# Values of a sliding-window attention: projected once per block of 128 tokens and copied to the overlapping key windows by DMA, instead of projected again for every window

## The chip, the core and the metric

The kernel runs on one core of a Trainium2 chip. The core has five engines that run side by side and meet only at semaphores: TensorE (PE, with its weight loads as PEld), VectorE (DVE), ScalarE (ACT), GpSimd (POOL) and SyncE (SP), which here only issues DMAs. Each engine works through its own instruction list in order, so an instruction that waits holds up everything behind it on that engine. The metric is the device time of one execution in microseconds (us), the median of several executions.

## The reference, cut to what matters

One transformer block with adaptive layer norm, 2048 tokens of 448 values, 16 heads of 28, bf16 inputs and outputs. Each token attends to itself and seven earlier tokens, two apart.

```python
mod = silu(c) @ w_mod                       # six rows of 448: sa, ca, ga, sb, cb, gb
h = layernorm(x) * (1 + ca) + sa
q, k, v = split(h @ wqkv)                   # 16 heads of 28
idx = pos[:, None] - arange(8) * 2          # masked where negative
o = softmax(q . k[idx] * 28**-0.5) . v[idx]
x = x + ga * (o @ wo)
h = layernorm(x) * (1 + cb) + sb
y = layernorm(h)
x = x + gb * (gelu(y @ w1 + b1) @ w2 + b2)  # hidden width 1792
```

## The kernel before, in words

**Layout.** Even tokens come first and odd tokens after them, so that the window of eight becomes eight neighbouring rows. The 2048 rows are 16 blocks of 128. `T.h` holds the normalized and modulated input transposed (four overlapping slices of the 448 channels on the partitions, tokens along the free axis), `T.q` and `T.k` the queries and keys in the same way.

**Attention.** Queries are cut into 36 groups of 57. A group needs 57 + 7 = 64 keys, so the key windows of neighbouring groups overlap by seven rows. Four groups make a *duo* (nine duos, `attention(d)`, line 676). In a duo, `lt` (line 694) multiplies keys and queries of all heads, `ex` (line 704, ACT) takes the exponential out of PSUM, `mk` (line 711, DVE) multiplies with a banded mask, `dn` (line 770) sums the weights, `pv` (line 783) multiplies them with the values, `ln` and `rc` (lines 793 and 798, ACT) make the reciprocal of the sum, and `on` (line 807, DVE) writes the result over the queries.

**Values before.** `v{d}` (lines 736 and 745) projects the values of a duo's four key windows straight onto the partitions where `pv` wants them: the window of 64 tokens is the stationary operand, so a matmul fills 64 of the 128 PSUM partitions, and two of them run beside each other at `tile_position=(0, 64 * u)`. That is 12 matmuls of 64 columns over 128 channels and 4 over the odd 64 channels, for two PSUM banks. `ve{d}.0` and `ve{d}.1` (line 294 through the helper `copy`, ACT) copy the two banks to the buffer `vb`, in which every head has 32 columns, of which the last four are zeroed once (`ebuf`). There are three `vb` buffers.

**The rest.** `qk` (lines 617 and 624, in `pair_mm`) projects queries and keys in pieces of 512 tokens. Blocks 0 to 7 are transposed by TensorE (`zt`, line 557), blocks 8 to 15 by a DMA transpose on SP (line 549). `wo` (line 823) and `x1` (line 832) add the attention to `x`; `norm2` makes the second and third layer norm on DVE, with a power on POOL (line 858) and an addition on POOL (`xp`, line 844), and transposes by DMA on SP (line 889). `w1` (lines 617 and 624), `gelu` (line 916, ACT), `w2` (line 929, the last block line 935) and `out` (line 946, DVE) are the MLP.

**The end.** The last block of 128 tokens is made in two halves of 224 columns, both in one PSUM tile, each with its own `out` and its own store (line 955).

**The start.** ACT issues three DMAs (part of `x`, two parts of `w_mod`), loads its function table and helps with the silu of `c`. POOL zeroes the padding and `wo`, makes the identity, the band mask (`mask1`) and its 16-fold copy (`mask`). `wo` has to be zeroed because only 28 of every 32 partitions are loaded. `fill` (line 466) are 28 matmuls of zeros which the planner puts wherever TensorE has nothing else.

**What sets the order.** Nothing is ordered by hand. Each piece of work is an item with its engine or engines, its dependencies and the buffers that it takes (`add`, line 77); PSUM is one pool of eight banks, `hm` one of three large buffers. `Plan.schedule` (line 107) plays the items through and, among those that can start, takes the one of highest priority; the priorities are a table of numbers per kind (`bias`) and per item (`delta`). The instruction list of each engine is the result. `phases` says which duos come before which quarters of the MLP: duos 0 to 6, quarters 0 and 1, duos 7 and 8, quarters 2 and 3. The exponential and the gelu need different ACT function tables, so ACT changes the table once per phase.

Of the kernel before, what the change touches and what calls it, by code (L numbers as in the profile page):

```python
# [66 lines left out]
class Plan:  # L67
# [162 lines left out]
CFG["tail"], CFG["slope"], CFG["window"] = 0.1512, 1.2963, 0.1  # L230
CFG["bias"] = {
    "bce": (-437.49, 11.669),
    "cst": (-315.02, 0.41),
    "dn": (-121.05, 0.55),
    "exp": (-590.42, 6.137),
    "gelu": (-217.98, 4.043),
    "h2": (-373.89, 0.036),
    "ln": (-583.27, 3.374),
    "lt": (72.47, 0.028),
    "md": (-377.14, 16.518),  # L240
    "mk": (54.22, 21.918),
    "mod2": (136.71, 0.694),
    "nm1": (32.99, 2.86),
    "nm2": (561.76, 2.811),
    "on": (169.44, 1.376),
    "out": (-413.48, 11.238),
    "pow1": (525.86, 1.379),
    "pow2": (-535.44, 0.028),
    "pv": (556.28, 40.0),
    "qk": (42.43, 17.816),  # L250
    "qke": (-395.64, 6.656),
    "rc": (-297.53, 6.437),
    "st1": (-388.63, 23.021),
    "st2": (24.1, 0.032),
    "store": (-563.5, 0.024),
    "v": (-393.34, 0.501),
    "ve": (573.27, 0.813),
    "w1": (-419.51, 24.455),
    "w2": (-582.63, 0.624),
    "w2s": (-527.88, 0.154),  # L260
    "wcp": (-38.96, 0.377),
    "wo": (-44.33, 40.0),
    "wos": (69.62, 2.823),
    "x1": (-248.35, 0.156),
    "xp": (-81.8, 6.268),
    "yt": (364.44, 0.134),
    "zt": (161.08, 0.071),
    "ztp": (-538.07, 0.138),
# [15 lines left out]
def build_plan(cfg):  # L284
# [13 lines left out]
    def memset(e, ap, c):  # L298
        T.eng[e].memset(ap, c)  # L299

    def psf(v):
        return T.ps[v.slot]

    def psb(v):
        return T.psb[v.slot]


    def fn(e):
# [5 lines left out]
    def load(name, nbytes, fn, wr, vals=(), n=1, q="SP", lag=0, lat=0.9, hold=()):  # L314
# [6 lines left out]
        it = add(name, "load", {q: 0.45 * n}, fn1, wr=wr, vals=vals, land=(lat, nbytes), after=after + list(hold))  # L321
        loads.append(it)
        return it
# [17 lines left out]

    def load_x(b0, n, q="SP", lag=0):
        def fn(e):
            return e.dma_start(out=T.x[:, b0:b0 + n, :], in_=xsrc(b0, n))
        return load(f"ldx{b0}", n * 128 * 896, fn, [("x", b) for b in range(b0, b0 + n)], q=q, lag=lag)

    def overl(dst, src, j, c0, c1):
        return dict(out=dst[:, 2 * j:2 * j + 2, 0:c1 - c0],
                    in_=src[192 * j:192 * j + 256, c0:c1].rearrange("(i p) n -> p i n", p=128))

    def fn(e):
        return e.dma_start(out=T.c_row[:], in_=T.c)
    load("ldc", 2000, fn, ["c_row"])
    load_x(0, 2, q="ACT")
    for i in range(3):
        def fn(e, i=i):
            w = wmod1()
            if i == 0:
                return e.dma_start(out=w[:, 0:2, :], in_=T.w_mod[0:256, 0:896].rearrange("(i p) n -> p i n", p=128))
            if i == 1:  # L360
                return e.dma_start(out=w[:, 3, :], in_=T.w_mod[320:448, 0:896])
            return e.dma_start(out=w[64:128, 2, :], in_=T.w_mod[256:320, 0:896])
        load(f"ldwmod1{i}", (256, 128, 64)[i] * 896 * 2, fn, [("wmod1", i)], vals=[fv], q=("SP", "ACT", "ACT")[i], lat=1.8)
    for j in range(2):
        def fn(e, j=j):
            return e.dma_start(**overl(T.Wv, T.wqkv, j, 896, 1344))
        load(f"ldwv{j}", 256 * 896, fn, [("Wv", j)])
    for j in range(2):
        def fn(e, j=j):
            return e.dma_start(**overl(wraw(), T.wqkv, j, 0, 896))  # L370
        load(f"ldwqk{j}", 256 * 896 * 2, fn, [("wraw", j)], vals=[fv])
    load_x(2, 2)
    load_x(4, 4)
    load_x(8, 4)
    for hh in range(2):
        for j in range(2):
            def fn(e, hh=hh, j=j):
                return e.dma_start(**overl(wmod2()[:, :, 896 * hh:896 * hh + 896], T.w_mod, j, 896 + 896 * hh, 1792 + 896 * hh))
            load(f"ldwmod2{hh}{j}", 256 * 896 * 2, fn, [("wmod2", hh, j)], vals=[wv], lag=3)
    for r in range(4):  # L380
        def fn(e, r=r):
            return e.dma_start(out=T.wo[32 * r:32 * r + DH, :, :],
                               in_=T.wo_d.rearrange("(m r e) n -> r e m n", r=4, e=DH)[r])
        load(f"ldwo{r}", 112 * 896, fn, [("wo", r)], lag=3)
    load_x(12, 4, lag=3)

    def fn(e):
        return e.dma_start(out=T.b1r[:], in_=T.b1.rearrange("(f p) -> f p", p=128))
    load("ldb1", 3600, fn, ["b1r"])

    def fn(e):
        return e.dma_start(out=T.b2[:], in_=T.b2_d.partition_broadcast(128))
    load("ldb2", 128 * 896, fn, ["b2"], lag=3)

    def fn(e):
        memset(e, T.zero[:], 0.0)
    add("zero", "cst", {"DVE": 0.3}, fn, wr=["zero"])

    def fn(e):
# [41 lines left out]
    def fn(e):  # L441
        memset(e, T.mask1[:], 1.0)
        for u in range(2):
# [4 lines left out]
                                      base=0, channel_multiplier=1)  # L448
    add("mask1", "cst", {"POOL": 1.0}, fn, wr=["mask1"])

    def fn(e):
        T.eng[e].tensor_copy(out=T.mask[:].rearrange("p (g c) -> p g c", c=SC),
                             in_=T.mask1[:].unsqueeze(1).to_broadcast([128, 16, SC]))
    add("mask", "cst", {"POOL": 1.0}, fn, rd=["mask1"], wr=["mask"])

    def fn(e):
        for t in T.vb:
            memset(e, t[:, :, :, DH:32], 0.0)
    add("ebuf", "cst", {"POOL": 0.9}, fn, wr=["ebuf"])


    fvl = val("ps", "fill")
    prev = None
    for i in range(cfg["nfill"]):
# [211 lines left out]
    def attention(d):  # L676
# [46 lines left out]
        def fn(e):  # L723
# [3 lines left out]
            def pos(P_, u):  # L727
                k0 = PADL + sub_tok(subs[P_][u]) - (WIN - 1)
                return k0
# [435 lines left out]
```

## Time and profile before

| what | us |
|---|---|
| median of three executions (lowest and highest) | 178.26 (177.97 to 179.09) |
| the profiled execution, its own time | 178.68 |
| its span, from the first to the last instruction | 177.0 |
| TensorE busy | 167.6 |
| DVE busy | 118.9 |
| ACT busy | 109.6 |
| POOL busy | 42.3 |

The profiled execution took 1.68 us more than its span, and 0.42 us more than the median. How to read the rows below: `ps<-Wv,hT` means that the tile `ps` (PSUM) was written from `Wv` and `hT`; `x108` is a count; a row of a timeline begins with the start and the length in us; what stands in brackets is how long the engine sat idle before it and what released it. The chain of waits is followed back from the last instruction to whatever released each one, and its rows give start and length in us. A busy TensorE is an upper bound, since the ends of pipelined matmuls are modelled, so its pace is better read from the distance of starts.

### The profile page before, as it was taken

Reading aid. Unit: us, or ns where it says so; the run is one execution under the profiler, and the core shown is the slowest. Engines: PE = TensorE matmul, PEld = TensorE weight load, DVE = VectorE, ACT = ScalarE, POOL = GpSimd, SP = SyncE. Lnnn points to the kernel's source line nnn. Section 1 sums busy time; section 2 is a strip of 40 time slices with the busy share of each in tenths; the row PEclk is TensorE's granted clock in tenths of the full one; section 3 lists DMA queues with packets and bytes.
Section 4 is the critical chain, followed back from the end, with each engine's and each line's share of the span. In section 5 each row is a group of like instructions: output and inputs, shape, how many; then the busy total and the mean of one; then the engine's idle time right before and its main releaser. Section 6 shows DMA issues by size and latency. Waiting matters only on the chain.

```text
span 177.0 us, 5323 instructions
## 1 busy us (share of the span) xinstructions
PE 167.6 (95%) x2243; PEld 83.3 (47%) x2243; DVE 118.9 (67%) x323; ACT 109.6 (62%) x203; POOL 42.3 (24%) x65
## 2 busy tenths in 40 slices
PE   7799996999899979999999999999999999999992
PEld 2457654344444453554434455555534455444571
DVE  3897898968989998999999906622785842200041
ACT  3077999969989987975567997802017820358100
POOL 7811320320415321101311102244241114200000
PEclk9999999999999999999999999999999999999999
DMA  5998384147986002000410400000221111300011
GB/s 163 375 365 272 123 166 80 32 93 214 327 255 81 4 17 52 4 0 4 89 30 11 98 15 4 6 0 27 83 104 30 31 28 31 107 0 0 0 67 37
DMA packets 23790, 15.13 MB, mean 86 GB/s; under 512 B 13909, under 2 KB 23766, under 8 KB 23766
## 3 DMA queue, kind: packets, MB, share of 16 engines
q1 hardware_dynamic: 23270, 14.22, 29.4%
q10 hardware_dynamic: 496, 0.57, 1.0%
q8 instruction: 17, 0.28, 0.6%
q14 instruction: 7, 0.06, 0.1%
HBM read 9.81 MB, written 1.84 MB: 66 GB/s over the span
## 4 chain that ended last, share of the span: by engine, by line
PE 78%; DVE 13%; ACT 3%; issue 2%; DMA 2%; POOL 0%; DVEq 0%; ACTq 0%
PE ps L617 29%; PE ps L929 23%; PE ps L823 7%; PE ps L624 6%; PE ps L736 4%; DVE z L541 3%; PE ps L783 2%; PE ps L694 2%; DVE et L711 2%; DVE st L523 2%; DMA x_all<-in_A_x_dram 2%; PE ps L935 2%; DVE qT L807 1%; ACT hT L589 1%; PE ps L770 1%
## 5 line engine op out<-in xcount | busy, mean ns | idle before, releaser
L916 ACT ACTIVATE hm<-ps,b1c 128x512 bf16<-128x512 f32 x56 | 34.3, 692 | 30.5 <-PE ps L624 26.4
L929 PE MATMUL ps<-w,hm 128*128 128x448 bf16 x210 | 40.9, 353 | 0.0
L617 PE MATMUL ps<-hT,w 128*128 128x512 bf16 x168 | 38.3, 380 | 0.0
L946 DVE TENSOR_TENSOR x_all<-ps,xp 128x448 bf16<-128x448 f32 (+1 forms) x17 | 10.0, 595 | 32.6 <-PE ps L929 30.5
L929 PEld LDWEIGHTS <-hm 128*128 128x128 bf16 x210 | 20.2, 98 | 18.8
L844 POOL TENSOR_TENSOR xp<-x_all,gbb 128x448 f32<-128x448 bf16 x16 | 17.0, 1063 | 39.7 <-DVE x_all L946 27.1
L617 PEld LDWEIGHTS <-w 128*128 128x128 bf16 x168 | 15.8, 98 | 20.7 <-issue 3.0
L858 POOL TENSOR_TENSOR rs<-tv,nhalf 128x2 f32<-128x2 f32 x16 | 12.4, 778 | 48.7 <-DVE tv L853 48.7
L617 PE MATMUL ps<-hT,Wqk 128*128 128x512 bf16 (+1 forms) x120 | 23.5, 337 | 0.0
L704 ACT ACTIVATE et<-ps 128x464 bf16<-128x464 f32 x36 | 18.1, 573 | 1.5 <-PE ps L694 1.5
L617 PEld LDWEIGHTS <-Wqk 128*128 128x128 bf16 x120 | 10.8, 98 | 9.7 <-issue 2.3
L711 DVE TENSOR_TENSOR et<-et,mask 128x928 bf16<-128x928 bf16 x18 | 11.0, 635 | 6.3 <-ACT et L704 6.2
L823 PE MATMUL ps<-wo,qT 128*128 128x448 bf16 x64 | 14.2, 354 | 1.0 <-DVE qT L807 1.0
L807 DVE TENSOR_TENSOR qT<-ps,rec 128x456 bf16<-128x456 f32 x18 | 11.3, 630 | 4.0 <-ACT rec L798 2.7
L736 PE MATMUL ps<-Wv,hT 128*64 128x448 bf16 x108 | 11.9, 357 | 0.0
L530 POOL TENSOR_TENSOR rs<-tv,nhalf 128x2 f32<-128x2 f32 x8 | 6.4, 804 | 20.8 <-DVE tv L526 20.5
L793 ACT ACTIVATE rec<-ps 128x464 f32<-128x464 f32 x18 | 10.0, 556 | 2.1 <-PE ps L770 2.1
L798 ACT ACTIVATE rec<-rec 128x464 f32<-128x464 f32 x18 | 10.6, 591 | 0.5
L832 DVE TENSOR_TENSOR x_all<-ps,x_all 128x448 bf16<-128x448 f32 x16 | 9.7, 620 | 1.9 <-PE ps L823 1.5
L523 DVE BATCH_NORM_STATS2 st<-x_all 128x6 f32<-128x448 bf16 x16 | 9.2, 614 | 1.9 <-DMA x_all<-in_A_x_dram 1.9
L294 ACT CAST vb<-ps 128x448 bf16<-128x448 f32 x18 | 8.8, 554 | 1.7 <-PE ps L745 1.7
L466 PE MATMUL ps<-zero 128*128 128x512 bf16 x28 | 8.5, 434 | 1.3 <-DVE oz L299 1.3
(92 smaller groups left out, 198.8 us busy)
## 6 DMA issues: line engine op xcount, KB each, us to landing
w<-in_B_w_dram SPq DMA_DIRECT2D x6, 448.0 KB, 4.2
hm<-in_w_mod_dram SPq DMA_DIRECT2D x5, 448.0 KB, 4.9
x_all<-in_A_x_dram SPq DMA_DIRECT2D x3, 448.0 KB, 4.3
out_dram<-x_all SPq DMA_DIRECT2D x3, 448.0 KB
hm<-in_A_wqkv_dram SPq DMA_DIRECT2D x2, 448.0 KB, 5.9
w<-in_B_w_dram SPq DMA_DIRECT2D x2, 336.0 KB, 4.9
Wv<-in_A_wqkv_dram SPq DMA_DIRECT2D x2, 224.0 KB, 5.0
wo<-in_A_wo_dram SPq DMA_DIRECT2D x4, 98.0 KB
```

Source lines behind the costliest of these rows:

```text
L523: T.nc.vector.bn_stats(out=T.st[:, b, :], in_=T.x[:, b, :])
L617: nc.tensor.matmul(outs[o], lhsT=stat(o, sl, 0, 128), rhs=mov(o, sl, 0, 128), start=(i == 0 and not flip and o // 2 % nb == 0), stop=(i == ...
L624: nc.tensor.matmul(outs[o], lhsT=stat(o, sl, lo, lo + 64), rhs=mov(o, sl, lo, lo + 64), start=(flip and o // 2 % nb == 0), stop=(not flip ...
L704: T.nc.scalar.activation(out=T.et[ev.slot][:, r * 464:(r + 1) * 464], in_=psf(lv[r])[:, 0:464], func=ACT.Exp, scale=float(DH) ** -0.5)
L711: T.eng[e].tensor_tensor(out=t, in0=t, in1=T.mask[:], op=ALU.mult)
L736: nc.tensor.matmul(psf(vv[P_])[64 * u:64 * u + 64, 0:D], lhsT=T.h[:, sl, k0:k0 + SK], rhs=T.Wv[:, sl, :], start=(i == 0 and not flip), sto ...
L807: T.nc.vector.tensor_tensor(out=T.q[:, :, c0:c0 + 2 * SQ].rearrange("p m (a c) -> p m a c", a=2), in0=v4(psf(po[u])[:, 0:464]), in1=v4(T.r ...
L823: T.nc.tensor.matmul(psf(vs[a])[:, 0:D], lhsT=T.q[:, m, c0:c0 + 128], rhs=T.wo[:, m, :], start=(m == 0), stop=(m == 3))
L844: T.eng[e].tensor_tensor(out=T.xp[xpv[b].slot][:], in0=T.x[:, b, :], in1=T.gbb2[:], op=ALU.add)
L858: T.nc.gpsimd.tensor_tensor(out=T.rs2[i][:, bs[0]:bs[0] + 2], in0=T.tv2[i][:, bs[0]:bs[0] + 2], in1=T.nhalf[:, 0:2], op=ALU.pow)
L916: T.nc.scalar.activation(out=T.hm[hmv[q].slot][:, 512 * f:512 * f + 512], in_=psf(v)[:, 0:512], func=ACT.Gelu_apprx_tanh, bias=T.b1c[:, f: ...
L929: T.nc.tensor.matmul(psf(v)[:, 0:D], lhsT=T.hm[hmv[q].slot][:, 512 * f + 128 * (b % 4):512 * f + 128 * (b % 4) + 128], rhs=T.w2[:, f, :], ...
```

## The change

**Values once per block.** The projection leaves `attention`. For each pair of blocks, `v{p}` now multiplies 128 tokens at a time with the same `pair_mm` as the other projections (6 matmuls of 128 columns over 128 channels and 2 over 64 channels, eight pairs). `ve{b}` copies each bank, 448 columns without gaps, to `vraw`, which takes one of the three large `hm` buffers. Then `vs{d}.{b}` on SP moves the rows to the `vb` buffer of each duo, one DMA for each stretch of rows that lies in one block: 52 DMAs of 1 to 64 rows of 896 bytes. `vb` has no gaps between heads now; `pv` reads 32 columns from the head's start, and the four superfluous ones are the next head's. `ebuf` zeroes all of `vb` once.

**Zeros and mask on ACT.** `woz` and `mask` go from POOL to ACT, as copies. `zero`, which `woz` reads, is made on DVE as before.

**Last block.** Its two parts are 288 and 160 columns, in two PSUM banks.

**Table of numbers.** `tail`, `slope`, `window`, `hold`, `margin`, `pen`, all of `bias` and all of `delta` are new; `phases`, `nfill`, `gq` and `g1` stay. One part of `w_mod` is loaded by SP instead of ACT, and `on` of duo 4 gets a dependency of its second half on its first.

```diff
-CFG["tail"], CFG["slope"], CFG["window"] = 0.1512, 1.2963, 0.1
+CFG["tail"], CFG["slope"], CFG["window"] = 0.0666, 1.5182, 0.03
...
-        memset(e, T.wo[:], 0.0)
-    add("woz", "cst", {"POOL": 1.0}, fn, wr=[("wo", r) for r in range(4)])
+        copy(e, T.wo[:, 0:2, :], T.zero[:, 0:D].unsqueeze(1).to_broadcast([128, 2, D]))
+        copy(e, T.wo[:, 2:4, :], T.zero[:, 0:D].unsqueeze(1).to_broadcast([128, 2, D]))
+    woz = add("woz", "cst", {"ACT": 1.7}, fn, rd=["zero"], wr=["woz"])
...
+        copy(e, T.mask[:].rearrange("p (g c) -> p g c", c=SC), T.mask1[:].unsqueeze(1).to_broadcast([128, 16, SC]))
+    add("mask", "cst", {"ACT": 1.0}, fn, rd=["mask1"], wr=["mask"])
...
-            memset(e, t[:, :, :, DH:32], 0.0)
+            memset(e, t[:].rearrange("p a c -> p (a c)").bitcast(FP32), 0.0)
...
+    vraw = val("hm", "vraw")
+    for p in range(NB // 2):
+        P.pos = 2.0 * p
+        vs = [val("ps", f"v{p}{i}") for i in range(2)]
+        def fn(e, p=p, vs=vs):
+            pair_mm([psf(v)[:, 0:D] for v in vs],
+                    lambda o, sl, lo, hi: T.h[lo:hi, sl, PADL + 256 * p + 128 * o:PADL + 256 * p + 128 * o + 128],
+                    lambda o, sl, lo, hi: T.Wv[lo:hi, sl, :])
...
+                copy(e, T.hm[vraw.slot][:, D * b:D * b + D], psf(v)[:, 0:D])
...
-        add(f"v{d}", "v" if d else "front", {"PE": 7 * MM[448] + 0.08}, fn,
...
+        for b in sorted(pieces):
+            def fn(e, b=b):
+                for P_, r, p0, n in pieces[b]:
+                    T.nc.sync.dma_start(out=T.vb[vbv.slot][r:r + n, P_, 0:D],
+                                        in_=T.hm[vraw.slot][p0:p0 + n, D * b:D * b + D])
...
-                                               lhsT=T.vb[vbv.slot][64 * u:64 * u + 64, P_, 4 * m + r, :],
+                                               lhsT=T.vb[vbv.slot][64 * u:64 * u + 64, P_, DH * (4 * m + r):DH * (4 * m + r) + 32],
...
+        halves = [(0, 288), (288, 448)] if last else [(0, 448)]
+        vs = [v, val("ps", f"o{b}b")] if last else [v, v]
```

How the instruction lists changed, at three places. The first is ACT's list from its start, before: three DMAs, the table, the exponential for the silu (`e_c`), the modulation of the first blocks.

```order
L344 DMA x_all<-in_A_x_dram 128x2x448
L361 DMA hm_78<-in_w_mod_dram 128x896
L362 DMA hm_78<-in_w_mod_dram 64x896
L416 ACT_TABLE_LOAD
L417 ACTIVATE warm<-nhalf 128x1
L479 ACTIVATE e_c<-ps_62 128x4
L589 ACTIVATE hT<-ps_64,mcol 128x256 x2
```

The same list in the changed kernel:

```order
L341 DMA x_all<-in_A_x_dram 128x2x448
L429 DMA hm_78<-in_w_mod_dram 128x896
L295 ACT_TABLE_LOAD
L295 COPY wo<-zero 128x896 x2
L375 ACT_TABLE_LOAD
L376 ACTIVATE warm<-nhalf 128x1
L480 ACTIVATE e_c<-ps_62 128x4
L295 COPY mask<-mask_111 128x928
L295 COPY silu_bc<-silu 128x128
L590 ACTIVATE hT<-ps_64,mcol 128x256 x2
```

Ahead of `e_c` there now stand a second table load and the two copies that zero `wo`, and one DMA less; the mask follows behind it.

The second place is SP's list around the loads of `w1` (`w_76`) and `w2` (`w_77`), before: the last transposes of the first layer norm, eight loads, the first transposes of the third layer norm.

```order
L549 DMA_TRANSPOSE hT<-z_91 128x4x128
L549 DMA_TRANSPOSE hT<-z_92 128x4x128
L578 DMA w_76<-in_B_w_dram 128x2x896 x4
L583 DMA w_77<-in_B_w_dram 128x4x448
L583 DMA w_77<-in_B_w_dram 128x3x448
```

And in the changed kernel, where `vb_85` is the value buffer of duo 2, `vb_86` that of duo 3, and `hm_80` is `vraw`:

```order
L550 DMA_TRANSPOSE hT<-z_92 128x4x128
L754 DMA vb_85<-hm_80 44x448
L754 DMA vb_85<-hm_80 1x16x28
L754 DMA vb_85<-hm_80 58x448
L754 DMA vb_85<-hm_80 64x448
L754 DMA vb_85<-hm_80 20x448
L579 DMA w_76<-in_B_w_dram 128x2x896 x3
L754 DMA vb_85<-hm_80 63x448
L754 DMA vb_85<-hm_80 6x448
L754 DMA vb_86<-hm_80 64x448
L754 DMA vb_86<-hm_80 34x448
L579 DMA w_76<-in_B_w_dram 128x2x896
```

Row moves for duos 2 and 3 now stand between the transposes and among the loads, two of duo 2 behind three loads of 448 KB.

The third place is ACT's list in the late attention of the changed kernel: `et_83` are the exponentials of duo 4, `rec_88` a reciprocal of duo 5, `et_81` the exponentials of duo 6, and `hm_80` the values of blocks 8 to 11.

```order
L724 ACTIVATE et_83<-ps_67 128x464
L724 ACTIVATE et_83<-ps_65 128x464
L724 ACTIVATE et_83<-ps_63 128x464
L724 ACTIVATE et_83<-ps_68 128x464
L789 ACTIVATE rec_88<-ps_61 128x464
L794 ACTIVATE rec_88<-rec_88 128x464
L295 CAST hm_80<-ps_62 128x448
L295 CAST hm_80<-ps_67 128x448
L724 ACTIVATE et_81<-ps_65 128x464
```

The values of blocks 8 and 9, which `pv` of duo 4 waits for through a row move, are copied out behind six other ACT instructions; TensorE's list has in the same place, in terms of items, `lt4 wo5 wo6 v4 lt6 v5 v6 pv4 dn4 dn6 v7`, where before it had `dn4 dn5 wo6 v5 wo7 dn6 v6 pv5 v7 pv6 v8`.

More of the change, by code (lines that the diff above doesn't have):

```diff
@@ L320, in fn1 @@
                 T.tc.add_manual_dep(it.ins.ins, a.ins.ins.name, SYNC, reason="one load after another")
-        it = add(name, "load", {q: 0.45 * n}, fn1, wr=wr, vals=vals, land=(lat, nbytes), after=after + list(hold))
+        it = add(name, "load", {q: 0.45 * n}, fn1, rd=rd, wr=wr, vals=vals, land=(lat, nbytes), after=after + list(hold))
         loads.append(it)
@@ L754, in attention @@
[L754 to L761 removed]
+        pieces = {}
@@ new lines, in attention @@
+        for i in range(4):
+            P_, u = i % 2, i // 2
+            r0, k0 = 64 * u, sub_tok(4 * d + i) - (WIN - 1)
+            lo, hi = max(k0, (4 * d + i) // 18 * SL), min(k0 + SK, (4 * d + i) // 18 * SL + SL)
+            while lo < hi:
+                b = lo // 128
+                n = min(hi, 128 * b + 128) - lo
+                pieces.setdefault(b, []).append((P_, r0 + lo - k0, lo - 128 * b, n))
+                lo += n
+        for b in sorted(pieces):
[3 more added lines that the diff above has]
+                                        in_=T.hm[vraw.slot][p0:p0 + n, D * b:D * b + D])
+            add(f"vs{d}.{b}", "vs", {"SP": 0.42 * len(pieces[b])}, fn, rd=[("vr", b), "ebuf"], wr=[("vb", d, b)],
+                vals=[vraw, vbv], land=(0.9, sum(x[3] for x in pieces[b]) * 896))
```

243 lines of the change are left out of this document (107 added, 136 removed).

## The prediction, made before the change was run

> **What bounds the kernel now.** I read the page's busy times first, then a table of stretches, then TensorE's waits, then the chain of waits. The page gives TensorE 95% of the span at full clock, and the row of slices shows where the rest is:
>
> ```profile
> PE 167.6 (95%) x2243; PEld 83.3 (47%) x2243; DVE 118.9 (67%) x323; ACT 109.6 (62%) x203; POOL 42.3 (24%) x65
> ...
> PE   7799996999899979999999999999999999999992
> ```
>
> The table of stretches has start and end, length, then the busy time of PE, PEld, DVE, ACT and POOL, the clock, the DMA share and GB/s:
>
> ```profile
> 10.30:29.40 19.10, 17.72 (x309) 10.91 (x309) 16.27 (x52) 16.98 (x37) 3.96 (x5) 1.00 0.72 198
> 29.40:66.10 36.70, 34.86 (x838) 16.71 (x838) 32.99 (x84) 33.55 (x67) 10.92 (x11) 1.00 0.48 125
> 66.10:102.60 36.50, 36.28 (x387) 15.94 (x390) 34.28 (x101) 27.01 (x47) 5.90 (x8) 1.00 0.18 38
> 128.00:173.50 45.50, 45.47 (x250) 22.19 (x248) 16.71 (x43) 17.20 (x28) 7.02 (x8) 1.00 0.14 40
> ```
>
> From 10.3 us on TensorE idles 1.38 + 1.84 + 0.22 + 0.03 us in these four stretches. So there are three parts: a start of 10.3 us, in which TensorE waits for its first real work; a body to 173.5 us, in which it has work nearly always, while DVE and ACT are about 90% busy up to 66 us and so are close seconds; and a tail of 3.5 us. Less TensorE work in the body is less time, unless new waits take its place. Its waits now, in us in total, times, longest:
>
> ```profile
> PE ps L694 <- DVE qT L807: 1.6, 2, 1.3
> PE ps L823 <- DVE qT L807: 1.0, 2, 0.7
> PE ps L783 <- issue: 0.5, 1, 0.5
> ```
>
> **Values once per block: the matmuls.** The chain of waits holds one whole projection of a duo and pieces of the same shapes as the new one:
>
> ```profile
> 10.35 1.26 PE ps L736 x12
> 11.60 0.31 PE ps L745 x4
> ...
> 35.54 0.32 PE ps L624 x2
> ...
> 36.47 1.40 PE ps L617 x6
> ...
> 141.25 10.59 PE ps L929 x56
> ```
>
> A duo costs 1.26 + 0.31 = 1.57 us, nine cost 14.1 us. A pair of blocks will take six matmuls of 448 columns and two over 64 channels. At the pace of L929 (10.59 / 56 = 0.189 us) six are 1.13 us; at that of L617 (1.40 us for six of 512 columns, times 448/512) they are 1.22 us. The two over 64 channels run side by side: 0.32 x 448/512 = 0.28 us. So 1.41 to 1.50 us a pair, 11.3 to 12.0 us for eight. The saving is 2.1 to 2.8 us; I take 2.5, as the w2 rows have the very width. It lies wholly on the engine that bounds.
>
> ACT loses two of 18 copies; the table also moves work off ACT and some off DVE. I cost this at nothing in the body, since both engines are only second there. The kept `vraw` buffer costs nothing as long as quarters 0 and 1 of the MLP have the other two large buffers, which `phases` allows.
>
> **The start.** Here two edits pull against each other.
>
> ```profile
> 5.23 0.77 POOL L530 TENSOR_TENSOR rs<-tv,nhalf 128x2 f32<-128x2 f32 x1 [0.26 <-DVE e_c L483]
> 5.88 1.62 POOL L299 MEMSET wo<- 128x1792 bf16 x1
> 7.44 1.01 POOL L452 COPY mask<-mask 128x928 bf16<-128x928 bf16 x1
> ```
>
> ```profile
> 6.03 2.57 DVE L541 TENSOR_SCALAR z<-x_all,mv,rs 128x512 bf16<-128x512 bf16 x2
> ...
> 13.61 0.73 DVE L541 TENSOR_SCALAR z<-x_all,mv,rs 128x512 bf16<-128x512 bf16 x2
> ```
>
> The first two normalizations take 2.57 us while POOL zeroes `wo` and copies the mask; the same pair takes 0.73 us later. With both moved to ACT, 1.84 us go from the path to the first transposes. But ACT's list has them ahead of the silu:
>
> ```profile
> 1.27 0.49 ACTq L361 DMA_DIRECT2D hm<-in_w_mod_dram  x1
> ...
> 2.35 1.28 ACT L416 ACT_TABLE_LOAD   x1 [2.35 <-issue]
> 3.64 0.20 ACT L417 ACTIVATE warm<-nhalf 128x1 f32<-128x1 f32 x1
> 4.23 0.17 ACT L479 ACTIVATE e_c<-ps 128x4 f32<-128x4 f32 x1 [0.38 <-PE ps L474]
> ...
> 9.89 1.49 ACT L294 COPY Wqk<-hm 128x448 bf16<-128x448 bf16 x3
> ```
>
> ACT will issue its second DMA until 1.76 us, load a table until 3.04, copy twice 896 columns (1.49 / 3 = 0.50 us for 448, so 2.0 us) until 5.0, load a table again until 6.3 and have `e_c` at 6.7 us instead of 4.4. On DVE the silu stands ahead of the normalizations:
>
> ```profile
> 5.05 0.16 DVE L483 TENSOR_SCALAR e_c<-e_c 128x4 f32<-128x4 f32 x1
> ...
> 5.54 0.16 DVE L485 TENSOR_TENSOR silu<-e_c,ps 128x4 bf16<-128x4 f32 x1
> ```
>
> ```profile
> 6.90 0.89 PE L499 MATMUL ps<-silu,hm 128*128 128x1 bf16 x30 [0.63 <-DMA hm<-in_w_mod_dram]
> ...
> 8.65 0.40 PE L557 MATMUL ps<-ident,z 128*128 128x128 bf16 x4 [0.56 <-DVE z L541]
> ```
>
> Silu ends 0.65 us after `e_c`, at 7.3 us, the normalizations at 8.1. TensorE makes the 32 modulation matmuls from 7.3 to 8.3 us, then a fill, four transposes, a fill, four transposes (about 0.2 us each), to 9.1 us; before it was 9.05. The first value projection then starts at 10.4 instead of 10.3 us. POOL's power is not in the way: without the mask copy and `wo` it still zeroes more of `vb`, but has until 7 us. Term: +0.1 us, from -0.5 (the start bound by the load of `w_mod`, 6.9 us) to +1.1 (copies half as slow again, with what follows them).
>
> **The tail.**
>
> ```profile
> 170.79 2.70 PE ps L935 x28
> ...
> 173.58 0.39 DVE x_all L946
> ```
>
> ```profile
> 173.58 0.69 DVE L946 TENSOR_TENSOR x_all<-ps,xp 128x224 bf16<-128x224 f32 x2 [2.13 <-PE ps L935]
> 174.00 0.82 SPq L955 DMA_DIRECT2D out_dram<-x_all  x2
> ```
>
> Both halves' additions start only after all 28 matmuls, at 173.58 us, although the first half was complete at about 172.1: they share a PSUM tile. With two banks the first addition and store run under the second part's matmuls. What follows the last matmul shrinks from two additions (0.69) and a queue of two stores to one addition of 160 columns (about 0.31, on the line through 0.38 for 224 and 0.62 for 448) and one store, issued at 173.9 instead of 174.4. Term: -0.5 us. The 28 matmuls keep their columns, so 2.7 us stay if they go by columns; if a matmul cannot go under 2.70 / 28 = 0.096 us, the 160-column ones cost 0.4 more. So -0.5 to -0.1.
>
> **The row moves and the new order.** No row of before shows an SBUF-to-SBUF DMA. Its neighbours are the stores and the DMA transposes, with their times from issue to landing:
>
> ```profile
> L955 SPq DMA_DIRECT2D out_dram<-x_all x7: 345/377/397, 122.6 to 174.4; - x7
> DMA to landing us min/median/max: 1.6/1.6/1.6
> ```
>
> ```profile
> L549 SPq DMA_TRANSPOSE hT<-z x8: 1191/1266/1979, 23.7 to 39.0; - x8
> DMA to landing us min/median/max: 2.4/3.4/5.0
> ```
>
> 52 moves at 0.38 us are 20 us of SP, which waits most of the body for DVE; POOL issues nothing. Behind a waiting move stand transposes of the next MLP quarter, but the order puts those 6 us or more ahead of their reader. The tight place is `pv` of duo 4. After its `lt`, ACT makes two copies, four exponentials, a logarithm and an exponential, and the first value copy:
>
> ```profile
> 64.15 1.91 ACT L704 ACTIVATE et<-ps 128x464 bf16<-128x464 f32 x4 [0.30 <-PE ps L694]
> ...
> 72.90 0.59 ACT L798 ACTIVATE rec<-rec 128x464 f32<-128x464 f32 x1
> 73.40 0.95 ACT L294 CAST vb<-ps 128x448 bf16<-128x448 f32 x2
> ```
>
> That is about 1.1 + 1.9 + 1.1 + 0.5 = 4.6 us; two moves are issued by 5.4 and land between 6.7 (at 1.6) and 8.5 (at 3.4). TensorE meanwhile has two `wo`, three projections and an `lt`, 1.7 + 4.3 + 0.6 = 6.6 us. So it waits 0 to 1.9 us; I take 1.0. For the two moves of duo 2 behind three loads, and for the first gelus, which ACT reaches about when TensorE runs out of banks, I take 1.3 together. Against these 2.3 us stand two old waits that lose their cause: `lt` of duo 1 (1.3) now has two projections between itself and the `on` that it waited for, and `wo` of block 5 (1.0) has `lt4` and two projections. Term: 0, from -2 (all old waits gone, no new one) to +4 (three places like duo 4's at their upper end).
>
> A rule of the Trainium skill speaks against the change here. The Trainium skill, "DMA: Bandwidth & Descriptors", section "Why a DMA increments its semaphore by 16 and not by 1", says that a DMA is spread over the largest number of engines up to 16 that divides its slowest dimension: 64 rows go to 16 engines, but 57 to three, 62 to two and 43 or 29 to one. No row of before can show it. By it the pieces with awkward row counts, about half, would land 1 to 2 us later, and I would add some 2 us to the sum.
>
> **Sum.** -2.5 (matmuls) + 0.1 (start) - 0.5 (tail) + 0 (waits) + 0.2 (one more fill after the first projection, eight against seven) = -2.7 us. Against the profiled execution's 178.68 this is 176.0; against the median, which is 0.42 lower, 178.26 - 2.7 = 175.6 us.
>
> **Rivals.**
>
> *The moves come late* (slower). A move waits for the value copy, then for its turn on SP, then lands; if landing takes 4 us or more in most places, `pv` of duos 1, 2, 4, 5 and 6 each hold TensorE for about 1.5 us and delay `on`, `wo` and the norms behind them. Five times 1.5 is 7.5 us, less the 1.3 or so already counted for them: 178.3 - 2.7 + 6.2 = about 182. It decides from the point where the new waits exceed the old ones by 4.5 us, since 178.26 - 2.7 + 4.5 is 1% slower. A price from rows: the main queue's packets, MB and share of 16 engines,
>
> ```profile
> q1 hardware_dynamic: 23270, 14.22, 29.4%
> ```
>
> take 0.294 x 16 x 177 us / 23270 = 36 ns for 611 bytes, so 896 bytes take about 52 ns, and 43 rows on one engine 2.3 us. For it: two pieces out of five are in a tight place. Against it: for duos 0, 1, 3, 5 and 6 the order has 5 to 12 us of TensorE work between the projection and `pv`. The rule of the Trainium skill named above ("DMA: Bandwidth & Descriptors") is what would make it so.
>
> *The saving comes back as waits* (within 1%). Up to 66 us DVE and ACT are busy 33.0 and 33.6 of 36.7 us. If they set the pace there, five of the projections save nothing, and new waits take about another 1: 178.3 - 0.5 - 2.5 x 4/9 + 1 = 177.6.
>
> *The start shortens too* (faster). If the second table load or the copies are quicker than costed, the 1.84 us on DVE come free up to the load of `w_mod`, -0.5, and if the old waits vanish too, -2: 175.6 - 2.5 = about 173.
>
> **How the numbers follow.** The forecast, 174.0 to 176.5: 0.56. The short start with vanished waits, under 174: 0.12. The saving comes back: 0.17. The moves come late: 0.15. Something of 1% (1.8 us) is about what a measurement of this kernel can tell from no change. So faster 0.68, same 0.17, slower 0.15. The range reaches from 173.4, the short start, into the third and the lower end of the late moves, 179.0; it leaves out about 0.05 below and 0.14 above.
>
> **What would show it.** Matmuls: the value rows of TensorE sum to starts about 1.45 us apart per pair, 64 instead of 144. Start: two table loads before `e_c`, the first pair of normalizations near 0.7 us, the first value projection near 10.4. Tail: an addition of 288 columns under the last matmuls, and one of 160 behind them. Moves: waits of TensorE at `pv` put down to a DMA, longest at duo 4, in sum about 2 us or less. The prediction is wrong if those waits pass 4 us, if moves land in 4 us or more, or if TensorE idles between 29 and 66 us for DVE or ACT by more than before.

## The result, and the profile after the change

The changed kernel takes 188.75 us (median of four executions, 187.77 to 189.14); the kernel before, run beside it, takes 178.12 us (177.89 to 179.09). The ratio is 1.058 (95% interval 1.052 to 1.064): slower by 10.6 us, where the prediction had 2.7 us faster. The profiled execution took 188.37 us, its span is 186.6 us. The ratios below leave out disturbed executions, more than 1.5% longer than the fastest of the same kernel, which the medians keep (one each of `six_later`, `by_need`, `late_moves` and `before_more_v`, four of six of `replan_pool`); the profiled one of `six_later` is such, so of its trace only the order of the waits is read.

The page's busy times, TensorE's row of slices and the row of its granted clock:

```profile
PE 170.9 (92%) x2163; PEld 82.4 (44%) x2163; DVE 116.4 (62%) x323; ACT 111.4 (60%) x205; POOL 41.6 (22%) x63
...
PE   6999699994999999949978999998999999999993
...
PEclk9999999999699999996999999999999999999999
```

DVE is busy 2.5 us less than before and ACT 1.8 us more, in a span that is 9.6 us longer. TensorE has two holes, in slices 10 and 18 of 40, and in the slice behind each the clock dips, to half speed from 47.0 to 50.4 and from 84.6 to 88.0 us. The table of stretches for the three stages up to 102.6 us:

```profile
10.30:29.40 19.10, 17.57 (x284) 10.53 (x281) 16.02 (x53) 15.17 (x33) 3.65 (x5) 1.00 0.81 213
29.40:66.10 36.70, 33.50 (x640) 15.24 (x638) 27.41 (x72) 29.43 (x60) 9.97 (x10) 0.95 0.58 147
66.10:102.60 36.50, 31.13 (x478) 13.61 (x477) 29.29 (x84) 23.91 (x45) 4.00 (x6) 0.95 0.21 51
```

TensorE idles 1.5 + 3.2 + 5.4 us here, against 1.4 + 1.8 + 0.2 before, and two stages run at a mean clock of 0.95: 5% of 36.7 us, 1.8 us, in each. Its longest waits:

```profile
PE ps L714 <- DVE qT L803: 2.8, 2, 2.6
PE ps L779 <- DMA vb<-hm: 2.7, 2, 2.3
PE ps L820 <- DVE qT L803: 2.5, 5, 0.6
...
PE ps L968 <- DMA hm<-in_w_mod_dram: 1.5, 1, 1.5
```

Only the second is a wait for a row move. The first is `lt` of duo 2 waiting for `on` of duo 1 on DVE. TensorE's row of it before:

```profile
42.14 0.70 PE L694 MATMUL ps<-qT,kT 28*64 28x58 bf16 x64 [0.29 <-DVE qT L807]
```

TensorE's row and DVE's rows at that place in the changed kernel:

```profile
46.55 0.74 PE L714 MATMUL ps<-qT,kT 28*64 28x58 bf16 x64 [2.58 <-DVE qT L803]
```

```profile
45.22 0.74 DVE L593 TENSOR_SCALAR hT<-hT,mcol 128x512 bf16<-128x512 bf16 x2 [2.83 <-DMA hT<-z]
45.87 0.63 DVE L803 TENSOR_TENSOR qT<-ps,rec 128x456 bf16<-128x456 f32 x1
```

DVE stands 2.83 us before a modulation that needs a DMA transpose of the first norm, with `on` next in its list. So the question is why the transpose is late. SP's issues before (start, length, count):

```profile
23.74 16.54 SPq L549 DMA_TRANSPOSE hT<-z  x8
40.32 4.06 SPq L578 DMA_DIRECT2D w<-in_B_w_dram  x4
```

and after:

```profile
24.10 1.31 SPq L550 DMA_TRANSPOSE hT<-z  x1
25.47 0.56 SPq L460 DMA_DIRECT2D b<-in_B_b_dram  x1
26.12 1.20 SPq L550 DMA_TRANSPOSE hT<-z  x1
27.58 6.32 SPq L754 DMA_DIRECT2D vb<-hm  x9
34.01 2.53 SPq L550 DMA_TRANSPOSE hT<-z  x2
36.63 1.46 SPq L754 DMA_DIRECT2D vb<-hm  x2
38.19 5.70 SPq L550 DMA_TRANSPOSE hT<-z  x4
...
75.22 10.73 SPq L754 DMA_DIRECT2D vb<-hm  x15
86.06 2.53 SPq L886 DMA_TRANSPOSE hT<-y  x2
```

From 24.1 to 43.9 us SP issues almost without a pause: eight transposes, eleven moves and the load of a bias. Before, the same transposes had 16.5 us to themselves and were out at 40.3 us. The second hole lies beside fifteen moves in a row, from 75.2 to 86.0 us: `pv` of duo 5 waits 2.27 us for one of them, and the next transposes of the third norm come at 86 us. What one move costs SP, as least, median and most in ns:

```profile
L754 SPq DMA_DIRECT2D vb<-hm x52: 498/648/862, 12.8 to 94.2; - x52
```

0.65 us, not 0.38; with the 0.06 us between two of them 52 moves are 37 us of SP, not 20.

### The profile page after: what moved, and what is told of

It reads as the page before. It is cut to its first block, busy times and chain, and to the rows that moved or that the text cites. A ratio compares the mean times of both kernels' runs of the same rounds, so it can differ in the third digit from the quotient of the medians.

```text
span 186.6 us, 5240 instructions
## 1 busy us (share of the span) xinstructions
PE 170.9 (92%) x2163; PEld 82.4 (44%) x2163; DVE 116.4 (62%) x323; ACT 111.4 (60%) x205; POOL 41.6 (22%) x63
## 5 line engine op out<-in xcount | busy, mean ns | idle before, releaser
L618 PE MATMUL ps<-hT,w 128*128 128x512 bf16 x168 | 40.3, 391 | 0.0
L946 DVE TENSOR_TENSOR x_all<-ps,xp 128x448 bf16<-128x448 f32 (+2 forms) x17 | 10.1, 596 | 33.2 <-PE ps L929 31.7
L841 POOL TENSOR_TENSOR xp<-x_all,gbb 128x448 f32<-128x448 bf16 x16 | 18.2, 1139 | 50.9 <-DVE x_all L946 29.5
L855 POOL TENSOR_TENSOR rs<-tv,nhalf 128x2 f32<-128x2 f32 x16 | 12.8, 797 | 54.7 <-DVE tv L850 54.7
L618 PE MATMUL ps<-hT,Wqk 128*128 128x512 bf16 (+1 forms) x120 | 24.0, 346 | 0.0
L724 ACT ACTIVATE et<-ps 128x464 bf16<-128x464 f32 x36 | 17.2, 572 | 2.8 <-PE ps L714 2.8
L820 PE MATMUL ps<-wo,qT 128*128 128x448 bf16 x64 | 15.2, 368 | 2.5 <-DVE qT L803 2.5
L618 PEld LDWEIGHTS <-Wqk 128*128 128x128 bf16 x120 | 11.1, 100 | 10.1 <-issue 3.8
L295 ACT CAST qT<-ps 128x512 bf16<-128x512 f32 x16 | 9.4, 596 | 6.3 <-PE ps L625 4.3
L531 POOL TENSOR_TENSOR rs<-tv,nhalf 128x2 f32<-128x2 f32 x8 | 5.8, 730 | 24.1 <-DVE tv L527 22.6
L467 PE MATMUL ps<-zero 128*128 128x512 bf16 x28 | 9.5, 462 | 1.8 <-DVE zero L300 1.8
L295 ACT CAST kT<-ps 128x512 bf16<-128x512 f32 x16 | 9.5, 592 | 2.6 <-PE ps L618 1.4
L779 PE MATMUL ps<-et,vb 64*32 64x58 bf16 x576 | 7.2, 192 | 3.9 <-DMA vb<-hm 2.7
```

What stands on the lines that cost most here:

```text
L295: T.nc.scalar.copy(out=out, in_=in_)
L618: nc.tensor.matmul(outs[o], lhsT=stat(o, sl, 0, 128), rhs=mov(o, sl, 0, 128), start=(i == 0 and not flip and o // 2 % nb == 0), stop=(i == ...
L724: T.nc.scalar.activation(out=T.et[ev.slot][:, r * 464:(r + 1) * 464], in_=psf(lv[r])[:, 0:464], func=ACT.Exp, scale=float(DH) ** -0.5)
L820: T.nc.tensor.matmul(psf(vs[a])[:, 0:D], lhsT=T.q[:, m, c0:c0 + 128], rhs=T.wo[:, m, :], start=(m == 0), stop=(m == 3))
L841: T.eng[e].tensor_tensor(out=T.xp[xpv[b].slot][:], in0=T.x[:, b, :], in1=T.gbb2[:], op=ALU.add)
L855: T.nc.gpsimd.tensor_tensor(out=T.rs2[i][:, bs[0]:bs[0] + 2], in0=T.tv2[i][:, bs[0]:bs[0] + 2], in1=T.nhalf[:, 0:2], op=ALU.pow)
```

## The experiments

Four theories. **Queue**: issuing moves fills SP's in-order list, and transposes and other moves behind them come late. **Landing**: `pv` waits for rows that are slow to land. **Order**: the new table of numbers is worse whatever the moves do. **Clock**: the dips of the clock are a cause of their own. Ratios are to the kernel before in the same batch of runs (177.5 to 177.7 us), with 95% intervals; the changed kernel's 1.058 is the ratio to compare with.

**Without the moves.** The DMA in the loop becomes `pass`.

> The changed kernel without its 52 row moves (the values are projected and copied to vraw, but pv multiplies with zeros; the attention output is left out of the result). Theory queue: the moves hold SP's in-order list at about 0.65 to 0.7 us each, so transposes and later moves are issued late, TensorE idles, and its clock drops behind the idle time. Theory landing: the moves are issued in time but land late. Theory order: the new table of numbers itself makes a worse order, moves or not. Queue and landing expect 175 to 177 us, which is the forecast of the prediction with no wait for a move; order expects 184 us or more.

177.52 us, ratio 1.0005 (0.9988 to 1.0022), half a us above what *queue* and *landing* expect. So the moves carry (1.0577 - 1.0005) or 0.057 x 177.6 = 10.2 us, and the order by itself is not slower than before: *order* falls as the cause. But no part of the forecast's 2.7 us is there either; that is taken up at the end. `lt` of duo 2 and of duo 7 in this run, against 46.55 and 113.30 us with the moves:

```profile
42.27 0.70 PE L714 MATMUL ps<-qT,kT 28*64 28x58 bf16 x64 [0.17 <-DVE qT L802]
...
102.05 0.70 PE L714 MATMUL ps<-qT,kT 28*64 28x58 bf16 x64
```

**Moves unread.** All moves are issued, and nobody waits for one.

```diff
-lhsT=T.vb[vbv.slot][64 * u:64 * u + 64, P_, DH * (4 * m + r):DH * (4 * m + r) + 32],
+lhsT=T.Wv[64 * u:64 * u + 64, P_, min(DH * (4 * m + r), 416):min(DH * (4 * m + r), 416) + 32],
```

> The changed kernel with all 52 moves issued in their places, but pv reads the weights Wv instead of the moved values (so the attention's values are left out), and nothing waits for a move to land. Queue theory (moves cost 0.65 us each of SP's list, and the transposes behind them come late): most of the 11 us that the moves cost stays, 184 to 187 us; only TensorE's 2.7 us of waits for moves at pv go, and the waits for DVE behind late transposes stay. Landing theory (pv holds TensorE until rows land, and on and wo are late for that): 177.5 to 180 us, near the 177.5 us without moves. Between 180 and 184 both have a share.

187.90 us, ratio 1.0587 (1.0561 to 1.0613), the same as with the waits, and above *queue*'s 184 to 187. *Landing* costs nothing that can be measured. The wait of 2.3 us at `pv` is gone, and the next reader of SP's list waits instead:

```profile
PE ps L618 <- DMA hT<-y: 3.5, 1, 3.5
PE ps L714 <- DVE qT L803: 3.4, 2, 3.0
```

**Moves from a constant.** As above, and `in_=T.Wv[p0:p0 + n, 0, :]`, so that no move waits for its source.

> As the run in which pv reads the weights, and besides, every move copies from the weights Wv, so that no move waits for a value copy either: SP pays only for issuing 52 moves (the attention's values are left out). If the issue time carries the price: 186 to 188.5 us, as with the waits. If it is moves that stand at the head of SP's list and wait for their value copy, with the transposes behind them: 178 to 181.

186.13 us, ratio 1.0484 (1.0448 to 1.0520). Of the 10.2 us 8.5 stay: in this order it is the issuing that costs, not moves that stand and wait with transposes behind them.

**GpSimd issues the moves.** `T.nc.sync.dma_start` becomes `T.nc.gpsimd.dma_start`, nothing else.

> The changed kernel with the 52 moves issued by GpSimd instead of SP; nothing else differs. Queue theory: SP's transposes are issued as early as before, the moves no longer stand behind transposes and loads, 178 to 182 us, unless an issue by GpSimd costs it so much that its own power and addition of the norms come late. Landing theory: rows land as late as before, 186 us or more.

179.39 us, ratio 1.0119 (1.0089 to 1.0148): 8.1 of the 10.2 us are gone. SP's transposes are out at 39.07 us (25.15 + 13.92), and GpSimd, which had room, pays 28.4 us. `lt` of duo 2 comes at 43.49 us, where it came at 46.55 with the moves on SP and at 42.27 without moves:

```profile
25.15 13.92 SPq L550 DMA_TRANSPOSE hT<-z  x7
```

```profile
43.49 0.70 PE L714 MATMUL ps<-qT,kT 28*64 28x58 bf16 x64 [0.76 <-DVE qT L803]
```

```profile
L754 POOL DMA_DIRECT2D vb<-hm x52: 505/542/738, 13.1 to 83.1; - x52
```

Together with the two runs before it this settles *queue*. The Trainium skill, "Perfetto Trace Analysis", section "What \"DMA-bound\" means", lists an issuing engine whose track is solid with DMA slices as a bound of its own. This case's trace agrees: SP's rows are solid from 24 to 44 us, and the DMA engines behind it were far from full (DMA share 0.58).

**Half of the moves.** `if not (d <= 3): continue` ahead of the move, or `d >= 4`.

> The changed kernel with the 24 moves of duos 0 to 3 alone; the 28 of duos 4 to 8 are left out (so the values of the later duos are not the attention's). The moves cost 11.2 us in all. Queue theory: the price comes at two places where SP issues without a pause, 24 to 44 us (duos 1 to 3, then the transposes of the first norm) and 75 to 86 us (duos 4 to 8); the gap and the dip of the clock behind it are alike in size, so 182 to 184 us here, with the gap at 45 us kept and the one at 80 us gone. If the late site carries nearly all: 178 to 180.

> The changed kernel with the 28 moves of duos 4 to 8 alone; the 24 of duos 0 to 3 are left out. Queue theory: 182 to 184 us, with the gap at 80 us kept and the one at 45 us gone, so that both halves together make the 11 us; if the two sites don't add up (a delay of the first is made good before the second), one half alone stands within 2 us of the whole, 187 or more.

184.03 us, ratio 1.0350 (1.0307 to 1.0392), and 185.09 us, ratio 1.0384 (1.0357 to 1.0412): 6.1 and 6.7 us, 12.8 together against 10.2. Both places have their price. The late half stands 1.1 us above its range of 182 to 184, and the sum overshoots by 2.6 us, so a part of the price seems to be shared; which part was not tried.

**Other orders of the moves on SP.** `by_need` puts the moves that are wanted first ahead of loads and of later moves (duo 2's ahead of three loads of `w1` and of duos 3 and 4, duo 5's ahead of duos 6 to 8); `six_later` puts three items (six moves) of duos 3 and 4 behind the last transpose of the first norm. The edit of `six_later`:

```diff
     order = P.schedule()
+    at = {it.name: it for it in order}
+    for names, mark in [(['vs3.7', 'vs4.7', 'vs3.6'], 'zt14')]:
+        for n in names:
+            order.remove(at[n])
+        i = order.index(at[mark]) + 1
+        order[i:i] = [at[n] for n in names]
```

> As six_later, and the moves of each later duo put in the order in which pv needs them (duo 2 ahead of the loads of w1, duo 5 ahead of a piece of duo 6, duo 6 ahead of duos 7 and 8). Queue expects both large gaps to close at least by half: 180 to 183 us. Landing and order expect 186 us or more.

184.38 us, ratio 1.0360 (1.0299 to 1.0421): above its 180 to 183, but 3.9 us better than the changed kernel with the same 52 moves.

> The changed kernel with six moves of duos 3 and 4 (blocks 6 and 7), which are not read until some 25 us later, put behind the last transpose of the first layer norm on SP's list; nothing else differs. Queue expects the wait of DVE for the transposes (2.8 us at 45 us) and that of TensorE behind it (2.6 us) to go, and the clock to stay up there: 4 to 5 us less, about 184. Landing and order expect no change beyond 1 us: 188.

194.86 us, ratio 1.0936 (1.0867 to 1.1005): a miss. The edit put the moves of duos 3 and 4 where those of duo 2 had been next, and `pv` of duo 2 stood behind them. The queue is in order, so whatever is moved past one reader's DMA lands on another's:

```profile
PE ps L779 <- DMA vb<-hm: 9.5, 3, 5.7
```

Both runs show besides that moves which wait are not free either. With the six gone from that place, SP waits for ACT to copy the values of the three moves that remain there; in `by_need` it issues nothing for 3.6 us, from 27.0 to 30.6, and the last transposes of the first norm are out at 42.9 us instead of 43.9. So most of the time that was taken out of the list came back as a wait in it.

**Matmuls of zeros against the dips of the clock.** Twelve ahead of `lt` of duo 2 and of `pv` of duo 5.

```diff
+            for i in range(12 if d == 2 else 0):
+                T.nc.tensor.matmul(psf(lv[i % 4])[:, 0:512], lhsT=T.zero[:, 0:128], rhs=T.zero[:], start=True, stop=True)
...
```

> The changed kernel with 12 matmuls of zeros ahead of lt of duo 2 and 12 ahead of pv of duo 5, into PSUM banks that these overwrite, so that TensorE works in the two long gaps without waiting less. Theory clock: the granted clock falls because TensorE idles over 2 us, and the slower matmuls behind the gaps are some 4 us of the loss; it expects 184 to 186 us and a granted clock of 1.00. If the clock is only a mark of the loss, the time stays at 188 to 190 us.

192.77 us, ratio 1.0837 (1.0769 to 1.0905), outside both expectations. The mean clock is 0.982 as before: the dips went elsewhere, to 99.5 to 106.3 us, and the run is 4 us slower at the same clock. This run does not show what causes a dip. What a dip costs is seen between executions of one kernel, and it differs: `by_need` took 182.99 and 183.63 us at clock 1.000 and 185.13 at 0.991, about 1.8 us for one dip; `replan_sp` (below) took 181.41 us at 1.000 and 182.48 to 182.70 at 0.981, about 0.6 us for each of two. The trace of the changed kernel has two dips, so, as an estimate from these figures, 1.2 to 3.6 of its 10.2 us come by way of the clock.

The kernel before ran at 0.996 or above in every execution beside the experiments, and kernels with long holes mostly did not. That the holes bring the dips is not shown, and the length of a hole does not decide: ahead of the changed kernel's dips TensorE works 0.8 and 1.6 of 3.4 us, while `before_less_v` (below) has a dip at 66.3 us behind 3.4 us in which it works 2.2, and none behind its hole of 2.1 us at 29.5. In every trace with dips a dip begins a whole number of steps of 3.41 us behind the first full clock, so where a hole falls on these steps may matter; no run tried it.

**The tail and the start alone, in the kernel before.** `before_tail` has the last block in two banks (the last lines of the change's diff). `before_tail_front` has besides `woz` and the mask on ACT, behind the first exponential.

> The kernel before with one part of the change: the last block in 288 and 160 columns in two PSUM banks. The prediction's term was -0.5 us (-0.5 to -0.1); the changed kernel's trace has 2.85 us behind the last matmul instead of 3.51, which makes -0.65. So 177.0 to 177.2 beside 177.6; 177.6 if the tail isn't what ends the run.

176.92 us, ratio 0.9964 (0.9951 to 0.9977): 0.64 us less (its own trace has 2.92 us behind the last matmul, that of the kernel before 3.50). This is faster than both kernels.

> The kernel before with the last block in two banks, and the zeroing of wo and the mask's copy moved to ScalarE behind the first exponential, so that no second table load stands ahead of it. If the normalizations, no longer slowed by GpSimd (2.57 us to 0.73), open the start: the first value projection 0.5 us earlier, which is bounded by the load of w_mod at 6.9 us, and 176.4 to 176.8 us together with the tail. If the load of w_mod and the modulation behind it bind the start already: 177.0 to 177.2, the tail alone.

176.88 us, ratio 0.9961 (0.9947 to 0.9975): no more than the tail alone, although the first value projection starts at 9.86 instead of 10.28 us:

```profile
9.86 1.33 PE L737 MATMUL ps<-Wv,hT 128*64 128x448 bf16 x12
```

Its first expectation (176.4 to 176.8) failed: the start is earlier by 0.42 us, and the end is not.

**The order made anew with the measured price.** The planner's price of a move becomes 0.71 on SP (or 0.55 on GpSimd, with the issuer changed), and the table of numbers is searched again with the planner's own forecast.

```diff
-        add(f"vs{d}.{b}", "vs", {"SP": 0.42 * len(pieces[b])}, fn, ...
+        add(f"vs{d}.{b}", "vs", {"SP": 0.71 * len(pieces[b])}, fn, ...
```

> The changed kernel with all 52 moves on SP, but the planner's price of a move 0.71 us (0.65 and the 0.06 between two of them) instead of 0.42, and the table of numbers made anew with that price. If the loss is an order made for a wrong price: 175 to 178 us, since the planner then keeps the transposes ahead of their readers. If 34 us of SP can't be had beside the transposes in any order: 181 us or more. The table is another in all its numbers, so a few tenths are not to be read.

182.29 us, ratio 1.0245 (1.0223 to 1.0267): 5.9 of the 10.2 us are gone with the same moves on the same queue, in another order (all numbers of the table differ, so this is not the price alone). Its expectation of 175 to 178 failed, and that of 181 or more holds. It stands 4.3 us above the changed kernel without moves; this order was not run without its own.

> The same with the 52 moves on GpSimd, at 0.55 us each in the planner's price, and the table made anew. 174.5 to 177 us if the saving of the matmuls (2 us) and of the tail (0.65 us) can both be had once SP is free of the moves; 177.5 or more if the order of the values itself (projections ahead of the duos that need them, on TensorE and ScalarE) gives the saving back, as the run without moves suggests.

187.87 us, ratio 1.0428 (1.0379 to 1.0476), which is 185.3 us. This table misses on the chip for other reasons (TensorE waits 3.4 us at an `lt` and 2.4 us at another), so the run says nothing on the saving. Whether an order exists in which values made once pay stays open.

**Is a matmul left out time gained?** In the kernel before, in its own order, the 36 value matmuls over 64 channels (L745) are left out, or made twice. The edit keeps `fulls()` alone with `start=(i == 0), stop=(i == 2)`, or runs the loop in `halves()` twice.

> The kernel before, in its own order, without the 36 value matmuls over 64 channels (those channels' part of the values is left out). Their starts take 2.70 us of TensorE in the trace of before. If TensorE bounds the body, as the prediction has it: 174.9 to 175.5 us beside 177.6. If ScalarE and VectorE set the pace up to 66 us, where five of the nine projections stand: about 176.4. If the saving is no time at all: 177.4 or more.

177.60 us, ratio 1.0012 (0.9990 to 1.0034): 2.7 us of TensorE work fewer, nothing gained, the third of its expectations.

> The same 36 matmuls made twice, in the same order (the values then hold that part twice). TensorE bound: 180 to 180.5 us. Bound by the others in the first half: about 178.8. No effect: 177.8 or less.

178.33 us, ratio 1.0043 (1.0028 to 1.0057): the rows of L745 take 1.7 us more, and the time grows by 0.8, between the second and the third of its expectations. TensorE's waits with less work and with more:

```profile
PE ps L694 <- DVE qT L802: 2.4, 2, 2.1
...
PE ps L818 <- DVE qT L802: 1.1, 2, 0.8
```

```profile
PE ps L823 <- DVE qT L807: 0.6, 2, 0.3
PE ps L694 <- DVE qT L807: 0.5, 2, 0.3
```

The kernel before has 1.6 and 1.0 there. `lt` waits for an `on` whose place in time DVE sets, not TensorE. At the longest of these waits DVE's rows of the kernel before, and then of the run with fewer matmuls:

```profile
27.58 0.63 DVE L997 TENSOR_TENSOR gbb<-gb,b 128x448 f32<-128x448 bf16 x1 [0.84 <-DMA b<-in_B_b_dram]
...
28.77 0.62 DVE L807 TENSOR_TENSOR qT<-ps,rec 128x456 bf16<-128x456 f32 x1
```

```profile
27.67 0.62 DVE L992 TENSOR_TENSOR gbb<-gb,b 128x448 f32<-128x448 bf16 x1 [1.20 <-DMA b<-in_B_b_dram]
...
28.86 0.63 DVE L802 TENSOR_TENSOR qT<-ps,rec 128x456 bf16<-128x456 f32 x1
```

DVE waits for the load of a bias, the `on` behind it runs at the same time in both, and what TensorE had saved by then is waited away. The same happens at 65 us, behind five of the nine projections, where DVE's rows follow each other almost without a pause from 57.9 to 65.9 us. The first `wo` that waits there, before and with fewer matmuls:

```profile
65.38 0.36 PE L823 MATMUL ps<-wo,qT 128*128 128x448 bf16 x1 [0.66 <-DVE qT L807]
```

```profile
65.35 0.36 PE L818 MATMUL ps<-wo,qT 128*128 128x448 bf16 x1 [0.82 <-DVE qT L802]
```

In half of the executions with fewer matmuls the clock is 0.99 besides; at 0.997 or above they take 177.1 to 177.4 us, so the saving there is some 0.3 us of 2.7.

## Why the prediction was wrong, point by point

**"Less TensorE work in the body is less time, unless new waits take its place."** This premise failed. It was read from TensorE's 95% of busy time. The matmuls did shrink: the value rows' starts sum to 12.0 us (9.96 + 2.08) instead of 14.0 (11.32 + 2.70), 2.0 us where 2.5 (2.1 to 2.8) was forecast. But `before_less_v` shows that 2.7 us of such work are worth 0 (at most 0.3). At 29 and at 65 us a load and DVE's own work set when `on` comes, and TensorE's idle time is what is left over, not a remainder to be used up. This was the rival *The saving comes back as waits*, whose case was in the row of stretches (DVE 33.0 and ACT 33.6 of 36.7 us); it should have had more than 0.17, and its "2.5 x 4/9" was too kind: the four later projections, 1.2 us of starts, were worth 0.3 us at most.

**"Term: 0" for the row moves and the new order.** This is the step that made the sign wrong: 10.2 us. Its working has two errors. "52 moves at 0.38 us are 20 us of SP" took the price of a store to DRAM; an SBUF-to-SBUF move costs SP 0.65 us. And SP, "which waits most of the body for DVE", was budgeted over the whole run. Between 23.7 and 40.3 us SP had eight transposes of 1.27 us, 10.1 of 16.5 us: 6.4 us of room, and eleven moves at 0.71 us need 7.8. This gives the direction and not the size: the transposes were out 4.8 us later than with the moves on GpSimd (43.9 against 39.1), and the room lay in pauses in which SP waited for DVE. The prediction looked at transposes of the next MLP quarter only behind a move that waits, not at those of the first norm behind moves that are merely issued.

**The tight place, `pv` of duo 4,** was the wrong place: the waits came at `lt` of duo 2 (by way of a transpose and DVE) and at `pv` of duo 5, while `pv` of duo 4 waits 0.5 us, for a value copy. The two old waits that were to vanish: that of `lt` of duo 1 is gone (0.2 us are left of L714's 2.8), and one of 2.6 us stands one duo later; `wo` waits 2.5 us instead of 1.0. Of the three signs by which the prediction was to be known as wrong, only the third is plain: TensorE idles 3.2 us between 29 and 66 us instead of 1.8. Its waits at `pv` for a DMA are 2.7 us, under the 4 that were named, and 45 of the 52 moves land in under 4 us from their issue.

***The moves come late*** had the right sign and the wrong mechanism: its 6.2 us were landing times at five `pv`. `unread` shows that these are worth nothing. The rule of the Trainium skill ("DMA: Bandwidth & Descriptors", section "Why a DMA increments its semaphore by 16 and not by 1") was cited for it. The trace agrees with its counts: the semaphore of a move of 62 rows is counted up by two engines, that of 43 rows by one and that of 64 rows by sixteen. The times are less apart: from the end of the issue the two moves of 62 rows land in 2.5 and 2.6 us, those of 43 rows in 2.8 and 4.6, and the sixteen of 64 rows in 1.4 to 4.3, half of them within 2.2. The 2 us that the prediction would have added by it were not paid, since landing is not what ends last.

**The start** went nearly as worked out: two table loads, `e_c` at 6.27 us (6.7 forecast), the pair of normalizations in 0.73 us, the first value projection at 10.20 (10.4):

```profile
1.77 1.28 ACT L295 ACT_TABLE_LOAD   x1 [1.77 <-PEq L1149]
3.07 1.78 ACT L295 COPY wo<-zero 128x896 bf16<-128x896 bf16 x2
4.86 1.28 ACT L375 ACT_TABLE_LOAD   x1
...
6.27 0.16 ACT L480 ACTIVATE e_c<-ps 128x4 f32<-128x4 f32 x1
```

That an earlier start would be time gained was wrong: `before_tail_front` starts 0.42 us earlier and ends no earlier.

**The tail** was right in its mechanism: -0.5 (-0.5 to -0.1) forecast, -0.64 measured alone, just beyond the better end. The first addition runs under the last matmuls, and one of 160 columns is left:

```profile
182.91 0.46 DVE L946 TENSOR_TENSOR x_all<-ps,xp 128x288 bf16<-128x288 f32 x1 [1.09 <-PE ps L936]
183.78 0.33 DVE L946 TENSOR_TENSOR x_all<-ps,xp 128x160 bf16<-128x160 f32 x1 [0.41 <-PE ps L936]
```

So of the sum -2.7 only the tail's part was time gained where it was tried alone. Without the moves even this is given back: `no_moves` has the tail and stands at 177.5. Its stretches from 66 to 128 us, and its longest wait:

```profile
66.10:102.60 36.50, 33.65 (x439) 14.92 (x441) 33.48 (x98) 26.05 (x46) 5.12 (x7) 1.00 0.15 30
102.60:128.00 25.40, 24.59 (x355) 11.71 (x345) 17.36 (x44) 15.78 (x28) 7.10 (x7) 1.00 0.06 13
```

```profile
PE ps L819 <- DVE qT L802: 2.8, 5, 0.6
```

TensorE idles 2.9 + 0.8 us there, where the kernel before idles 0.2 (in the two stretches ahead, from 10.3 us on, it idles 1.2 us against 3.2), and waits 2.8 us in all for an `on` just ahead of its `wo`. That the new order puts the two too close is argued from these rows and was not tried.

## What to carry to other kernels

An engine that only issues DMAs has a budget too: add up issue times for each stage, transposes and moves together, with the price of the very kind of DMA, and compare with the room in that stage, not in the run. A share of 95% on one engine doesn't show that leaving out its work gains time: leave some out, or double it, in the kernel as it is, before a change is built on it. And where a queue is in order, ask for each DMA that is put into it what stands behind it, not only who waits for it.

## What the runs showed of the hardware that was not expected

- An SBUF-to-SBUF DMA of 1 to 64 rows takes 0.50 to 0.86 us of SP's list. This goes less by its size than by the number of engines that count up its semaphore: 0.50 to 0.59 us for 64 or 48 rows on sixteen engines, 0.65 for 43 rows on one, 0.76 to 0.78 for 20 rows on ten, 0.86 for 15 rows on fifteen. The store of before took 0.38. GpSimd issues the same moves in 0.51 to 0.74 us, in the median 0.54.
- A copy on ACT ahead of the preload of the function table brings a table load of its own, 1.28 us; with the same copies behind the first exponential (`before_tail_front`) there is one load at the start.
- The granted clock of a one-core kernel dips in stretches of 3.4 us, at half speed, each worth 0.6 to 1.8 us of time; the same kernel has none in one execution and two in the next (`replan_sp`: 181.41 us at 1.000, 182.70 at 0.981).
